# Attention scores as two 64-row products on their own halves of TensorE's rows, in place of one 128-row product with block-diagonal keys

## The chip, the cores and the metric

One NeuronCore of a Trainium2 chip runs the whole program in one launch. The metric is the time of one execution on the device in microseconds (us). The kernel before takes 1839.62 us, the median of 3 runs (1839.45 to 1840.44).

## The reference

Attention over 8 batches of 8 heads with keys and values averaged over groups of 8 positions, then two channel-mixing layers of width 512 to 2048 to 512. Only the attention scores are touched by the change.

```python
# B, H, S, D = 8, 8, 576, 64; pool = 8; Sp = 72
k_p = k.reshape(B, H, Sp, pool, D).mean(axis=3)
v_p = v.reshape(B, H, Sp, pool, D).mean(axis=3)
scores = scale * np.matmul(q, k_p.transpose(0, 1, 3, 2))     # per head: [576, 64] x [64, 72]
scores = scores - np.max(scores, axis=-1, keepdims=True)
attn = np.exp(scores)
attn = attn / (np.sum(attn, axis=-1, keepdims=True) + 1e-09)
x = np.matmul(attn, v_p)                                     # then heads side by side: [8, 576, 512]
h = x.transpose(0, 2, 1) @ U @ V
u = x + h.transpose(0, 2, 1)
x = u + np.maximum(u @ w_ch1, 0.0) @ w_ch2                   # first layer
...
out = x + np.maximum(norm(x) @ w_ch1, 0.0) @ w_ch2           # second layer
```

## The kernel before

The program has two parts. Phase A (`phase_a`) runs the attention of all 8 batches and, one batch behind it, half of the first layer's mixing (`a_l1`, L1015, and `a_l2`, L1047, 24 and 24 groups of main matmuls at L1027 and L1060, 288 columns each). Then three passes over 9 groups of 512 tokens run the rest of the mixing (matmuls at L1257 and L1345).

Attention goes by pairs of heads, 4 pairs per batch, 32 in all. The two heads of a pair lie one above the other: rows 0 to 63 of a tile are the 64 dimensions of the first head, rows 64 to 127 those of the second. For each pair `att_load` (L696) brings q, k and v; `att_prep` (L710) sums the keys over 8 positions into `kp` [128, 72], on VectorE (L718) or in three steps on GpSimd (L721, L722), and copies each head's half of `kp` into its own block of `kbd` [128, 2, 72], whose other blocks are zeros since the start (L494). The two copies run on ScalarE or VectorE. `att_s` (L759) then makes the scores of 128 queries with both heads in one product: 128 queries of both heads are the stationary operand (a weight load of 128 columns), `kbd` with its 144 columns streams past, and 128 x 144 scores land in PSUM (L767). Five such products make a pair, three in a first bank of the ring `py` and two in a second.

`att_m` (L775) takes the maxima (L789), scales them (L797), runs ten exponentials on ScalarE (L803) and divides by the sums. `att_t` (L820) turns the result back with TensorE transposes (L378): two blocks of four with 128 rows, and one of two with 64 rows, from rows 64 to 127, for the last 64 queries. `att_av` (L854) multiplies with the values (L871, or L889 and L890 from the third batch on). `att_xt` (L902) and `att_g` (L920) transpose the heads' outputs and multiply them with U (L927 and L928), in five steps of which the last has 64 rows only.

No order is written out by hand across engines. Every operation is recorded with the engines that can run it and its cost there, and `schedule` (L151) plays these through and hands out engine and place by due time; the program is emitted in that order and each engine then runs its own list in that order. For TensorE the due time is a running sum of planned costs. The scores' planned cost is one line:

```python
            {PE: 4 * 2 * SP / 2.4},
```

The ring `py` has 4 PSUM banks, and scores, transposes, the products with V, U and the rest of the attention share them. The rings `kbd`, `kp` and `q` have two tiles each.

Of the kernel before, what the change touches and what calls it, by code (L numbers as in the profile page):

```python
# [14 lines left out]
ALU = mybir.AluOpType  # L15
AX = mybir.AxisListType
# [7 lines left out]
SP = S // POOL  # L24
# [12 lines left out]
QT = [0, 128, 256, 384, 448]  # L37
# [54 lines left out]
PE, ACT, DVE, GP, SY = "pe", "act", "dve", "pool", "sync"  # L92
# [253 lines left out]
def c_dve(n):  # L346
    return 68 + 1.042 * n


def c_fast(n):  # L350
    return 68 + 0.521 * n


def c_act(n, ps=False):
    return (51 if ps else 93) + 0.8333 * n


def c_pool(n):
    return 147 + 2.11 * n
# [21 lines left out]
def copy(nc, e, dst, src):  # L381
    if e is nc.scalar:
        e.copy(dst, src)  # L383
    else:
        e.tensor_copy(dst, src)  # L385


class Kern:
    def __init__(self, nc, tc, aps):
        self.nc, self.tc = nc, tc  # L390
        (self.qT, self.kT, self.v, self.U, self.V, self.wA, self.g, self.wC, self.out) = aps
        self.w_raw = [self.wA, self.wC]
        self.o = Order(nc, tc)
        att = Pool("att")
        stg = Pool("stg")
        slots = Pool("slots", side="right")
        w = Pool("wres", side="right")
        b1 = Pool("b1", after=[att])
        b2 = Pool("b2", side="right", after=[w])
        ps = Pool("ps", space=PSUM)  # L400
        self.pools = [stg, att, slots, w, ps, b1, b2]
        R = self.R = {}

        def ring(pool, name, shape, dt=F32, n=1, fifo=True):
            R[name] = Ring(pool, shape, dt, n, name, fifo)

        ring(stg, "wraw", [128, 512], I64)
        ring(stg, "wx", [128, 512])
        ring(stg, "wt", [128, 512])
        ring(att, "araw", [128, 512], I64)  # L410
        ring(att, "ax", [128, 512])
        ring(att, "at", [128, 512])
        ring(att, "kbd", [128, 2, SP], n=2)
        ring(att, "q", [128, S], n=2)
        ring(att, "k", [128, S])
        ring(att, "v", [SP, 2, POOL * D])
        ring(att, "kp", [128, SP], n=2)
        ring(att, "vs", [SP, 4, D], F32R, 3)
        ring(att, "vz", [SP, 3 * D], n=2)
        ring(att, "ef", [SP, 2, S])  # L420
        ring(att, "sc", [128, 5, 2 * SP], n=2)
        ring(att, "mx", [128, 10], n=2)
        ring(att, "sm", [128, 10], n=2)
        ring(att, "eh", [SP, 2, S], F32R)
        ring(att, "el", [SP, 2, S], F32R)
        ring(att, "avt", [128, SH], n=2)
        ring(att, "xT", [128, S], n=5)
        ring(att, "xh", [128, DM], F32R, 2)
        ring(att, "xl", [128, DM], F32R, 2)
        ring(att, "gr", [128, DM], F32R)  # L430
        ring(att, "gs", [128, DM], F32R)
        ring(att, "ust", [128, 5, 128], F32R)
        ring(att, "vstk", [128, S], F32R)
        ring(slots, "op", [128, SLOT], F32R, 16)
        ring(slots, "hid", [128, SLOT], F32R, 8)
        for f in range(NA):
            for a in "hl":
                ring(w, f"w{a}{f}", [128, 1024], F32R)
        ring(w, "ys", [128, SH], n=2)
        for j in range(NSL):  # L440
            pool = b1 if j < NSL - 1 else b2
            for a in "hl":
                ring(pool, f"w1{a}{j}", [128, 7, 256], F32R)
                ring(pool, f"w2{a}{j}", [128, 2, 512], F32R)
        ring(b1, "xraw", [128, NCC, TG])
        ring(b1, "t3", [128, 2, TH])
        ring(b1, "t2", [128, 2, TH])
        ring(b2, "s12", [128, TG], n=2)
        ring(b2, "s5", [128, TH], n=2)
        ring(b2, "res", [128, NCC, TG], n=2)  # L450
        ring(b2, "yt", [128, NCC, TG])
        for a in ("lnh", "lnl"):
            ring(b2, a, [128, TH], F32R)
        for a in ("lns", "lnq", "lnm", "lnv", "lnd"):
            ring(b2, a, [128, TH])
        ring(ps, "pa", [128, 512], n=2)
        ring(ps, "pbc", [128, 512], n=2, fifo=False)
        ring(ps, "py", [128, 512], n=4)
# [31 lines left out]
                self.w_d[layer, f] = dp.tile([128, 1024], F32, tag=f"w_d{layer}_{f}", name=f"w_d{layer}_{f}")  # L490

    def setup2(self):
        for t in self.R["kbd"].tiles:
            self.nc.gpsimd.memset(t, 0.0)  # L494
        for t in self.R["vz"].tiles:
            self.nc.gpsimd.memset(t[:, D : 2 * D], 0.0)

# [212 lines left out]
    def att_prep(self, P):  # L710
        nc, o = self.nc, self.o
        q, k, v = self.raw[P]
        kp, kbd = self.buf("kp"), self.buf("kbd")
        kv = lambda: k.t.rearrange("p (n s) -> p n s", s=POOL)

        def pool(e):
            if e is nc.vector:
                e.tensor_reduce(kp.t, kv(), axis=AX.X, op=ALU.add)  # L718
                return
            for n in (4, 2):  # L720
                e.tensor_add(kv()[:, :, :n], kv()[:, :, :n], kv()[:, :, n : 2 * n])  # L721
            e.tensor_add(kp.t, kv()[:, :, 0], kv()[:, :, 1])  # L722

        o.op({DVE: c_dve(S), GP: c_pool(4 * SP) + c_pool(2 * SP) + c_pool(SP)}, pool, w=[k, kp])
        for h in range(2):
            r = slice(64 * h, 64 * h + 64)
            o.op(
                {ACT: c_act(SP), DVE: c_fast(SP)},
                lambda e, r=r, h=h: copy(nc, e, kbd.t[r, h], kp.t[r]),
                r=[kp],  # L730
                w=[(kbd, h)],
            )
        self.qk[P] = (q, kbd)

    def att_prep_v(self, P):
        o = self.o
# [20 lines left out]
        )  # L757

    def att_s(self, P, t):  # L759
        q, kbd = self.qk[P]  # L760
        if t in (0, 3):
            self.sps[P, t // 3] = self.buf("py")
        ps = self.sps[P, t // 3]
        i = t % 3 * 2 * SP
        self.o.op(
            {PE: 4 * 2 * SP / 2.4},
            lambda e: e.matmul(  # L767
                ps.t[:, i : i + 2 * SP], q.t[:, QT[t] : QT[t] + 128], kbd.t.rearrange("p h n -> p (h n)"),
                start=True, stop=True, skip_group_check=True,
            ),  # L770
            r=[q, kbd],
            w=[ps],
        )

    def att_m(self, P):  # L775
        nc, o = self.nc, self.o
        self.sc[P] = self.buf("sc")
        sb, mx, sm = self.sc[P], self.buf("mx"), self.buf("sm")
        sc = lambda: sb.t.rearrange("p t (h n) -> p (t h) n", h=2)
        bc = lambda t: t.rearrange("p (g o) -> p g o", o=1).to_broadcast([128, 10, SP])  # L780
        n = 10 * SP
        both = {GP: 1350, DVE: c_dve(n)}
        scale = 1.0 / (POOL * 8)
        for z, (g0, g1) in enumerate(((0, 6), (6, 10))):
            ps = self.sps[P, z]
            m = (g1 - g0) * SP
            o.op(
                {DVE: c_dve(m)},
                lambda e, ps=ps, g0=g0, g1=g1, m=m: e.tensor_reduce(  # L789
                    mx.t[:, g0:g1], ps.t[:, :m].rearrange("p (g n) -> p g n", n=SP), axis=AX.X, op=ALU.max  # L790
                ),
                r=[ps],
                w=[(mx, z)],
            )
            o.op(
                {DVE: 74, GP: 170},
                lambda e, g0=g0, g1=g1: e.tensor_scalar(mx.t[:, g0:g1], mx.t[:, g0:g1], -scale, None, op0=ALU.mult),  # L797
                w=[(mx, z)],
            )
            for g in range(g0, g1):  # L800
                o.op(
                    {ACT: 297},
                    lambda e, ps=ps, g=g, g0=g0: e.activation(  # L803
                        sc()[:, g],
                        ps.t[:, (g - g0) * SP : (g - g0 + 1) * SP],
                        AF.Exp,
                        bias=mx.t[:, g : g + 1],
                        scale=scale,
                        accum_out=sm.t[:, g : g + 1],
                    ),  # L810
                    r=[ps, (mx, z)],
                    w=[(sb, g), (sm, g)],
                )
        o.op(
            {DVE: 74}, lambda e: e.tensor_scalar(sm.t, sm.t, 1e-9, float(POOL), op0=ALU.add, op1=ALU.mult), w=[sm]
        )
        o.op({DVE: 131}, lambda e: e.reciprocal(sm.t, sm.t), w=[sm])
        o.op(both, lambda e: e.tensor_mul(sc(), sc(), bc(sm.t)), r=[sm], w=[sb])
# [788 lines left out]
```

## Time and profile before

| what | before |
|---|---|
| median of 3 runs | 1839.62 us (1839.45 to 1840.44) |
| profiled execution: its own time | 1839.23 us |
| profiled execution: span | 1837.4 us |
| TensorE matmul busy | 1769.2 us (96%), 11482 records |
| TensorE weight loads busy | 1619.5 us (88%) |
| VectorE busy | 1279.1 us (70%) |
| ScalarE busy | 723.4 us (39%) |
| GpSimd busy | 435.6 us (24%) |
| mean granted TensorE clock | 0.977 |
| the chain that ended last, by engine | PE 87%, DVE 9%, DMA 1%, ACT 1% |

PE is TensorE's matmul side and PEld its weight loads, DVE is VectorE, ACT ScalarE, POOL GpSimd. An f32 matmul instruction shows as two records on PE and two on PEld; one of another type as one. The end of a matmul record is modelled, and successive matmuls overlap in the records, so the length of a record (0.29 us for a score product) is not what it costs: that is read from how far the ends of successive records stand apart.

### The profile page before, as it was taken

How to read it: one execution, taken by the hardware profiler on the slowest of the kernel's cores; microseconds unless marked ns; L12 is line 12 of the kernel's file. 1: busy time of each engine (PE TensorE's matmuls, PEld its weight loads, DVE VectorE, ACT ScalarE, POOL GpSimd, SP SyncE). 2: the span in 40 equal slices, each digit the busy share in tenths (PEclk: the TensorE clock that was granted, in tenths of full speed). 3: DMA queues.
4: the chain of work that ended last, by engine and by line, in shares of the span. 5: the costliest groups of instructions: out<-in, count | busy, mean ns of one | idle time of the engine just before them, and what ended most of it. 6: DMA issues, size and time to landing. Idle time of an engine off the chain costs nothing.

```text
span 1837.4 us, 30175 instructions
## 1 busy us (share of the span) xinstructions
PE 1769.2 (96%) x11482; PEld 1619.5 (88%) x11482; DVE 1279.1 (70%) x2512; ACT 723.4 (39%) x2047; POOL 435.6 (24%) x446
## 2 busy tenths in 40 slices
PE   5689999999999999999999999999999999999999
PEld 4579999999999998888888888999999999999998
DVE  7987888888855577888888898776434754454443
ACT  4445655655644233333333453333332432222221
POOL 2242322323310122222222331111111321111110
PEclk7689999999999999999999999999999999999999
DMA  6434444444411352333333334434111433222211
GB/s 179 152 114 154 137 153 155 138 154 149 124 62 46 111 192 81 115 115 115 115 115 115 115 127 138 132 127 142 53 64 58 160 116 115 93 92 92 98 64 47
DMA packets 88642, 212.42 MB, mean 116 GB/s; under 512 B 9264, under 2 KB 17456, under 8 KB 82736
## 3 DMA queue, kind: packets, MB, share of 16 engines
q1 hardware_dynamic: 88352, 210.49, 34.8%
q8 instruction: 90, 1.47, 0.3%
q14 instruction: 56, 0.46, 0.1%
q10 hardware_dynamic: 144, 0.00, 0.0%
HBM read 141.25 MB, written 69.21 MB: 115 GB/s over the span
## 4 chain that ended last, share of the span: by engine, by line
PE 87%; DVE 9%; DMA 1%; ACT 1%; issue 1%; POOL 0%; SPq 0%; DVEq 0%; ACTq 0%; POOLq 0%
PE py L1345 30%; PE pa L1257 15%; PE pbc L1257 12%; PE pa L1027 11%; PE pbc L1060 10%; PE py L378 3%; PE py L767 2%; PE py L871 1%; DVE lnv L1468 1%; DVE res L1481 1%; DVE lnd L1466 1%; PE py L889 1%; PE py L890 1%; PE py L928 0%; DMA v<-v 0%
## 5 line engine op out<-in xcount | busy, mean ns | idle before, releaser
L1345 PE MATMUL py<-hid,w2h 128*128 128x512 f32 x1728 | 546.4, 398 | 0.0
L1257 PE MATMUL pa<-op,w1h 128*128 128x256 f32 x1728 | 328.5, 282 | 21.5 <-DVE pa L1321 19.8
L1257 PEld LDWEIGHTS pa<-op,w1h 128*128 128x128 f32 x1728 | 294.0, 189 | 59.4 <-DVE pa L1321 22.6
L1345 PE MATMUL py<-hid,w2l 128*128 128x512 f32 x864 | 337.9, 391 | 0.0
L1345 PEld LDWEIGHTS py<-hid,w2h 128*128 128x128 f32 x1728 | 278.7, 191 | 13.4
L1257 PE MATMUL pbc<-op,w1h 128*128 128x256 f32 x1296 | 247.2, 283 | 1.3 <-ACT s L383 0.6
L1257 PEld LDWEIGHTS pbc<-op,w1h 128*128 128x128 f32 x1296 | 221.9, 190 | 28.5 <-DVE lnv L1465 0.8
L1257 PE MATMUL pa<-op,w1l 128*128 128x256 f32 x864 | 244.2, 283 | 0.0
L1027 PE MATMUL pa<-hid,wh 128*128 128x288 f32 x1024 | 220.1, 307 | 8.9 <-DVE op L1039 8.8
L1060 PE MATMUL pbc<-op,wh 128*128 128x288 f32 x1024 | 215.8, 303 | 0.0
L1315 DVE TENSOR_TENSOR pbc<-s,pbc 128x512 f32<-128x512 f32 x108 | 74.8, 692 | 183.2 <-PE pbc L1257 183.1
L1345 PEld LDWEIGHTS py<-hid,w2l 128*128 128x128 f32 x864 | 163.4, 189 | 36.6
L1257 PE MATMUL pbc<-op,w1l 128*128 128x256 f32 x648 | 183.7, 283 | 0.0
L1027 PEld LDWEIGHTS pa<-hid,wh 128*128 128x128 f32 x1024 | 167.1, 192 | 12.3 <-DVE op L1039 8.7
L1279 ACT ACTIVATE hid<-pbc 128x512 fp32r<-128x512 f32 x108 | 64.7, 599 | 266.4 <-DVE pbc L1315 265.6
L1060 PEld LDWEIGHTS pbc<-op,wh 128*128 128x128 f32 x1024 | 163.7, 188 | 4.4 <-issue 2.8
L1257 PEld LDWEIGHTS pa<-op,w1l 128*128 128x128 f32 x864 | 163.4, 189 | 0.0
L1027 PE MATMUL pa<-hid,wl 128*128 128x288 f32 x512 | 153.3, 299 | 0.4 <-POOL wl L508 0.4
L1060 PE MATMUL pbc<-op,wl 128*128 128x288 f32 x512 | 150.9, 295 | 0.0
L383 ACT COPY s<-pa 128x256 f32<-128x256 f32 x200 | 74.3, 372 | 146.3 <-PE pa L1257 144.1
L508 POOL TENSOR_TENSOR op<-t,op 128x512 fp32r<-128x512 f32 x26 | 35.2, 1356 | 393.0 <-DVE op L385 312.5
L1279 ACT ACTIVATE hid<-pa 128x512 fp32r<-128x512 f32 x108 | 64.5, 597 | 156.3 <-PE pa L1257 149.4
(189 smaller groups left out, 3135.3 us busy)
## 6 DMA issues: line engine op xcount, KB each, us to landing
xraw<-n_d SPq DMA_DIRECT2D x18, 1024.0 KB, 4.8
wraw<-wC SPq DMA_DIRECT2D x32, 512.0 KB, 4.1
wraw<-wA SPq DMA_DIRECT2D x24, 512.0 KB, 4.3
w_d<-wx SPq DMA_DIRECT2D x48, 256.0 KB, 4.0
wraw<-w_d SPq DMA_DIRECT2D x48, 256.0 KB, 3.7
k<-kT SPq DMA_DIRECT2D x32, 288.0 KB, 3.7
q<-qT SPq DMA_DIRECT2D x32, 288.0 KB, 3.2
v<-v SPq DMA_DIRECT2D x32, 288.0 KB
```

The lines of the kernel that those rows point to most:

```text
L378: e.matmul(out, src, ident, start=first, stop=True, is_transpose=True, skip_group_check=True)
L383: e.copy(dst, src)
L508: lambda e: e.tensor_sub(lo(), src(), hi().bitcast(F32)),
L767: lambda e: e.matmul(ps.t[:, i : i + 2 * SP], q.t[:, QT[t] : QT[t] + 128], kbd.t.rearrange("p h n -> p (h n)"), start=True, stop=True, ski ...
L871: lambda e: e.matmul(ps.t[:, :SH], vs.t[:, w], ef.t[:, h, c], start=(h == 0), stop=(h == 1)),
L889: e.matmul(ps.t[:, :SH], w, eh.t[:, h, c], start=True, stop=False)
L1027: e.matmul(ps.t[:, :SH], w.t[:, c], u, start=(i == 0), stop=(i == 3 * NCC - 1))
L1060: e.matmul(ps.t[:, :SH], w.t[:, c], x, start=(f == 0 and j == 0), stop=(f == NA - 1 and j == 2))
L1257: e.matmul(bank.t[:, sl], w.t[:, self.WCOL[k], c], u.t[:, t], start=(first and i == 0), stop=(last and i == 5), skip_group_check=True,)
L1279: lambda e: e.activation(h.t[:, :TG], bank.t, AF.Relu),
L1315: o.op({DVE: c_dve(TG)}, lambda e: e.tensor_add(c.t, s.t, c.t), r=[s], w=[c])
L1345: e.matmul(y.t, w.t[:, i, c], x.t[:, :TG], start=(first and q == 0), stop=(last and q == 2))
```

## The change

The zero blocks and the copies into them go. `att_s` issues two products for each 128 queries, one per head. Each has the head's 64 rows of q as its stationary operand (still 128 columns) and the head's 64 rows of `kp` as the streaming one (72 columns), the second head's on rows 64 to 127 of TensorE. The two heads write into two different banks, both taken from the ring at the pair's first product, so that a bank holds the five blocks of one head and not three or two blocks of both heads. `att_m` reads them so: each bank's maxima go to every second column of `mx`. The planned cost of a score product becomes 3 * 72 / 2.4 = 90 ns, two of them 180 ns, where one of 240 ns stood.

```diff
-        ring(att, "kbd", [128, 2, SP], n=2)
...
     def setup2(self):
-        for t in self.R["kbd"].tiles:
-            self.nc.gpsimd.memset(t, 0.0)
...
-        kp, kbd = self.buf("kp"), self.buf("kbd")
+        kp = self.buf("kp")
...
-        for h in range(2):
-            r = slice(64 * h, 64 * h + 64)
-            o.op(
-                {ACT: c_act(SP), DVE: c_fast(SP)},
-                lambda e, r=r, h=h: copy(nc, e, kbd.t[r, h], kp.t[r]),
-                r=[kp],
-                w=[(kbd, h)],
-            )
-        self.qk[P] = (q, kbd)
+        self.qk[P] = (q, kp)
...
     def att_s(self, P, t):
-        q, kbd = self.qk[P]
-        if t in (0, 3):
-            self.sps[P, t // 3] = self.buf("py")
-        ps = self.sps[P, t // 3]
-        i = t % 3 * 2 * SP
-        self.o.op(
-            {PE: 4 * 2 * SP / 2.4},
-            lambda e: e.matmul(
-                ps.t[:, i : i + 2 * SP], q.t[:, QT[t] : QT[t] + 128], kbd.t.rearrange("p h n -> p (h n)"),
-                start=True, stop=True, skip_group_check=True,
-            ),
-            r=[q, kbd],
-            w=[ps],
-        )
+
+        q, kp = self.qk[P]
+        if t == 0:
+            self.sps[P] = self.buf("py"), self.buf("py")
+        for h, ps in enumerate(self.sps[P]):
+            r = slice(64 * h, 64 * h + 64)
+            self.o.op(
+                {PE: 3 * SP / 2.4},
+                lambda e, r=r, ps=ps: e.matmul(
+                    ps.t[:, t * SP : t * SP + SP], q.t[r, QT[t] : QT[t] + 128], kp.t[r],
+                    start=True, stop=True, skip_group_check=True,
+                ),
+                r=[q, kp],
+                w=[ps],
+            )
...
-        for z, (g0, g1) in enumerate(((0, 6), (6, 10))):
-            ps = self.sps[P, z]
-            m = (g1 - g0) * SP
+        for z in range(2):
+            ps = self.sps[P][z]
+            m = 5 * SP
...
-                    mx.t[:, g0:g1], ps.t[:, :m].rearrange("p (g n) -> p g n", n=SP), axis=AX.X, op=ALU.max
+                    mx.t[:, z:10:2], ps.t[:, : 5 * SP].rearrange("p (g n) -> p g n", n=SP), axis=AX.X, op=ALU.max
...
-            for g in range(g0, g1):
+            for g in range(z, 10, 2):
...
-                        ps.t[:, (g - g0) * SP : (g - g0 + 1) * SP],
+                        ps.t[:, g // 2 * SP : (g // 2 + 1) * SP],
```

Lines of the changed program from `att_s` on stand ten lower: the scores are L757, the main matmuls L1017 and L1050. On TensorE 160 score instructions become 320. The three places that follow show how they stand among the others; `hid` is a batch's input to the mixing, `wh` and `wl` its weights, `sc` the exponentials of a pair, `pa` and `pbc` the mixing's banks.

TensorE, a pair in the third batch, its last two score products and what stands around them, before:

```order
L767 MATMUL py_235<-kbd_144,q_146 128x144
L1060 MATMUL pbc_234<-op_197,wh_222 128x288 x2
L1060 MATMUL pbc_234<-op_197,wl_223 128x288
L1060 MATMUL pbc_234<-op_198,wh_224 128x288 x2
L1060 MATMUL pbc_234<-op_198,wl_225 128x288
L378 MATMUL py_237<-ident,sc_157 72x128 x4
L767 MATMUL py_235<-kbd_144,q_146 128x144
L1060 MATMUL pbc_233<-op_191,wh_210 128x288 x2
```

The same place in the changed program:

```order
L757 MATMUL py_233<-kp_148,q_144 128x72
L757 MATMUL py_234<-kp_148,q_144 128x72
L1050 MATMUL pbc_232<-op_195,wh_220 128x288 x2
L1050 MATMUL pbc_232<-op_195,wl_221 128x288
L1050 MATMUL pbc_232<-op_196,wh_222 128x288 x2
L1050 MATMUL pbc_232<-op_196,wl_223 128x288
L378 MATMUL py_235<-ident,sc_155 72x128 x4
L757 MATMUL py_233<-kp_148,q_144 128x72
L757 MATMUL py_234<-kp_148,q_144 128x72
L1050 MATMUL pbc_231<-op_189,wh_208 128x288 x2
```

One score product between 128-row work has become two 64-row ones that stand together, one per head.

TensorE, a later pair in the changed program, where the second head's products do not stand beside the first's:

```order
L757 MATMUL py_233<-kp_148,q_144 128x72
L378 MATMUL py_234<-ident,sc_155 72x128 x4
L757 MATMUL py_233<-kp_148,q_144 128x72 x2
L1017 MATMUL pa_230<-hid_201,wh_210 128x288
L1017 MATMUL pa_230<-hid_202,wh_210 128x288
L1017 MATMUL pa_230<-hid_201,wl_211 128x288
```

Here four transposes of 128 rows have moved in between the products of one head.

VectorE, the first rows of the program, before:

```order
L718 TENSOR_REDUCE kp_149<-k_147 128x72
L385 COPY kbd_143<-kp_149 64x72 x2
L747 TENSOR_TENSOR v_148<-v_148 72x2x256
L789 TENSOR_REDUCE mx_159<-py_235 128x6
L797 TENSOR_SCALAR mx_159<-mx_159 128x6
L789 TENSOR_REDUCE mx_159<-py_236 128x4
L797 TENSOR_SCALAR mx_159<-mx_159 128x4
```

and in the changed program:

```order
L715 TENSOR_REDUCE kp_147<-k_145 128x72
L736 TENSOR_TENSOR v_146<-v_146 72x2x256
L736 TENSOR_TENSOR v_146<-v_146 72x2x128
L779 TENSOR_REDUCE mx_157<-py_233 128x5
L779 TENSOR_REDUCE mx_157<-py_234 128x5
L787 TENSOR_SCALAR mx_157<-mx_157 128x5
L542 TENSOR_SCALAR at_142<-araw_140 128x512
```

The copies into `kbd` are gone from VectorE here, and one of the two scalings of the maxima has moved to GpSimd. Over the program 25 such copies leave VectorE and 39 leave ScalarE, and of the 32 sums of keys 20 now stand on GpSimd, 12 on VectorE (10 and 22 before).

## Rows read from the trace of the kernel before

**Rows 1.** Engines by stretch: us, busy (instructions) PE, PEld, DVE, ACT, POOL, clock, DMA, GB/s

```profile
0.00:140.00 140.00, 99.72 (x484) 83.44 (x485) 121.28 (x288) 64.46 (x262) 43.12 (x53) 0.77 0.49 147
140.00:600.00 460.00, 458.56 (x3406) 441.73 (x3405) 361.89 (x808) 252.60 (x912) 119.79 (x150) 1.00 0.41 128
600.00:1150.00 550.00, 527.22 (x3327) 478.61 (x3326) 442.89 (x807) 209.06 (x466) 152.57 (x147) 0.98 0.36 121
```

**Rows 2.** Waits of PE, 140 to 600 us (all): total us, times, longest us

```profile
PE py L928 <- DVE xl L508: 1.3, 3, 0.5
```

**Rows 3.** Waits of PE, 0 to 140 us, the three longest

```profile
PE py L378 <- DVE sc L818: 13.1, 3, 9.9
PE pa L1027 <- DVE op L1039: 8.8, 3, 5.9
PE py L767 <- DVE kbd L385: 5.0, 1, 5.0
```

**Rows 4.** Score products, 140 to 575 us: records, ns min/median/max, first and last start

```profile
L767 PEld LDWEIGHTS py<-kbd,q x232: 187/189/193, 141.0 to 559.5; 128*128 128x128 f32 x116
L767 PE MATMUL py<-kbd,q x232: 283/286/288, 141.1 to 559.6; 128*128 128x144 f32 x116
```

**Rows 5.** Timeline of PE around one score product: start us, us, what

```profile
202.53 0.29 PE L890 MATMUL py<-el,vs 72*128 72x288 f32 x1
202.66 0.41 PE L767 MATMUL py<-kbd,q 128*128 128x144 f32 x2
202.81 0.52 PE L1027 MATMUL pa<-hid,wh 128*128 128x288 f32 x2
203.17 0.29 PE L1027 MATMUL pa<-hid,wl 128*128 128x288 f32 x1
```

**Rows 6.** Timeline of PE, products with U on 128 rows

```profile
218.10 0.29 PE L1060 MATMUL pbc<-op,wl 128*128 128x288 f32 x1
218.23 0.40 PE L927 MATMUL py<-xh,ust 128*128 128x512 f32 x1
218.47 0.39 PE L928 MATMUL py<-xl,ust 128*128 128x512 f32 x1
218.69 0.60 PE L378 MATMUL py<-ident,xT 128*128 128x128 f32 x4
```

**Rows 7.** Timeline of PE, the same products on 64 rows

```profile
224.50 0.29 PE L1060 MATMUL pbc<-op,wl 128*128 128x288 f32 x1
224.72 0.50 PE L927 MATMUL py<-xh,ust 64*128 64x512 f32 x1
225.05 0.39 PE L928 MATMUL py<-xl,ust 64*128 64x512 f32 x1
225.38 0.53 PE L1060 MATMUL pbc<-op,wh 128*128 128x288 f32 x2
225.74 0.29 PE L1060 MATMUL pbc<-op,wl 128*128 128x288 f32 x1
```

**Rows 8.** Timeline of PE, transposes from rows 64 to 127

```profile
207.20 0.41 PE L767 MATMUL py<-kbd,q 128*128 128x144 f32 x2
207.54 0.30 PE L378 MATMUL py<-ident,sc 64*72 64x64 f32 x2
207.78 0.53 PE L1027 MATMUL pa<-hid,wh 128*128 128x288 f32 x2
208.14 0.29 PE L1027 MATMUL pa<-hid,wl 128*128 128x288 f32 x1
```

**Rows 9.** Copies into kbd, 0 to 140 us

```profile
L383 ACT COPY kbd<-kp x14: 247/249/254, 11.5 to 124.3; 64x72 f32<-64x72 f32 x14
L385 DVE COPY kbd<-kp x6: 181/192/196, 4.5 to 26.4; 64x72 f32<-64x72 f32 x6
```

**Rows 10.** Engines by stretch, as rows 1; and the longest wait of PE from 600 to 1150 us

```profile
750.00:800.00 50.00, 47.45 (x284) 42.59 (x285) 41.86 (x74) 18.29 (x42) 14.61 (x16) 0.95 0.38 127
...
PE pa L1257 <- DVE pa L1321: 19.8, 10, 2.4
```

More of the change, by code (lines that the diff above doesn't have):

```diff
@@ L783, in att_m @@
         scale = 1.0 / (POOL * 8)
-        for z, (g0, g1) in enumerate(((0, 6), (6, 10))):
-            ps = self.sps[P, z]
-            m = (g1 - g0) * SP
+        for z in range(2):
+            ps = self.sps[P][z]
+            m = 5 * SP
             o.op(
                 {DVE: c_dve(m)},
-                lambda e, ps=ps, g0=g0, g1=g1, m=m: e.tensor_reduce(
-                    mx.t[:, g0:g1], ps.t[:, :m].rearrange("p (g n) -> p g n", n=SP), axis=AX.X, op=ALU.max
+                lambda e, ps=ps, z=z: e.tensor_reduce(
+                    mx.t[:, z:10:2], ps.t[:, : 5 * SP].rearrange("p (g n) -> p g n", n=SP), axis=AX.X, op=ALU.max
                 ),
@@ L796, in att_m @@
                 {DVE: 74, GP: 170},
-                lambda e, g0=g0, g1=g1: e.tensor_scalar(mx.t[:, g0:g1], mx.t[:, g0:g1], -scale, None, op0=ALU.mult),
+                lambda e, z=z: e.tensor_scalar(mx.t[:, z:10:2], mx.t[:, z:10:2], -scale, None, op0=ALU.mult),
                 w=[(mx, z)],
             )
-            for g in range(g0, g1):
+            for g in range(z, 10, 2):
                 o.op(
                     {ACT: 297},
-                    lambda e, ps=ps, g=g, g0=g0: e.activation(
+                    lambda e, ps=ps, g=g: e.activation(
                         sc()[:, g],
-                        ps.t[:, (g - g0) * SP : (g - g0 + 1) * SP],
+                        ps.t[:, g // 2 * SP : (g // 2 + 1) * SP],
                         AF.Exp,
```

## The prediction

> **What bounds the kernel now.** I read the engines by stretch first [rows 1]. From 140 to 600 us TensorE is busy 458.56 of 460 us at a clock of 1.00; the same stretch shows VectorE at 362 and GpSimd at 120 us. Busy matmul records overlap, so the list of TensorE's waits must confirm it: in these 460 us it names one group of 1.3 us in all [rows 2]. So in this stretch whatever a score product costs TensorE more or less comes out at the end, one for one. Before 140 us it is otherwise: TensorE is busy 100 us at a clock of 0.77, VectorE 121, and TensorE waits mostly for VectorE [rows 3]. From 600 to 1150 us TensorE idles 23 of 550 us [rows 1].
>
> Next, what a score product costs. Records are 0.286 us long [rows 4], but their ends stand closer. From the end of L890 (202.53 + 0.29 = 202.82) to the end of the last main product (203.17 + 0.29 = 203.46) lie 0.64 us [rows 5]; three main products take 0.13 each (203.33 to 203.46 is one), which leaves 0.25 for the score instruction, 0.125 for each of its two records.
>
> Last, what 64 rows cost among 128-row work, which this kernel already has in two places. The two products with U take 0.47 us on 128 rows (ends 218.39 to 218.86) [rows 6]. On 64 rows the span from the end of the product before them (224.79) to the end of the third main product behind (226.03) is 1.24 us [rows 7]; take off 0.47 and 3 x 0.13 and 0.38 us are left over. The records show where: L927 ends 0.43 after its forerunner and not 0.24, and the main products behind stand 0.2 late. The two 64-row transposes show the same: from 207.61 to 208.43 are 0.82 us [rows 8]; less 0.39, and less 0.11 for two transposes of 64 columns (one of 128 columns takes 0.11: four end 0.43 after L928 [rows 6]), 0.32 us are left. Their weight load has 72 columns, that of L927 128, as the new score products have. So entering and leaving 64-row work costs TensorE 0.32 to 0.38 us each time, however much stands between.
>
> By the Trainium skill, page TensorEngine Tiling (Array Packing), Key Properties, changing the tiling mode drains TensorE, while another tile of the same mode does not. The 0.38 us agree with the first half; no run here yet shows the second.
>
> **The change part by part.** *Switches.* In the changed order I count runs of neighbouring 64-row products from the 193rd main product on, which is where the records of rows 4 begin. Before there are 33 (25 begin with transposes, 8 with a product with U or its correction): 25 x 0.32 + 8 x 0.38 = 11.0 us. After there are 122, of which 96 begin with a score, 18 with transposes, 8 with the others: 104 x 0.38 + 18 x 0.32 = 45.3 us. That is **+34.2 us**, all of it on TensorE's solid stretch. Score products that stand together share one switch, which is why it is 122 and not 230.
>
> *The products themselves.* In this stretch 117 score instructions become 230, each two records: 234 x 0.125 = 29.3 us become 460 records. If streaming sets their pace, 72 columns take half of 144, 0.0625 us: 28.8 us in all, -0.5. If the weight load sets it, the nearest row is the transposes with loads of 128 columns, 0.11 us apart [rows 6]; that row's streaming alone could set 0.11, so it is an upper bound. The first load of each of the 96 runs lies inside the switch, so 96 x 0.0625 + 364 x 0.11 = 46.0 us, +16.7. If the second record of one head runs beside the first of the other (they own different rows and banks), a pair of instructions takes three places of four: 21.6 us, -7.7. I take 0.085 us, half way between streaming and load, since neither row decides: 6.0 + 30.9 = 36.9, **+7.6 us**.
>
> By the Trainium skill, page TensorE: Matmul & The Clock Gate, section LDWEIGHTS, a weight load's time goes by its columns, whatever its rows, at 1/1.2 ns each: an estimate of 107 ns here, which makes the sum of the loads much like the bound just named; rows 6 do not contradict it.
>
> *Before 140 us* 17 runs stand where 8 stood: 9 x 0.38 is 3.4 us at the full clock and 6.8 at the half. TensorE is only part of what bounds this stretch, so perhaps half of that counts. Against it, 6 copies of 0.19 us leave VectorE and 14 of 0.25 leave ScalarE [rows 9], and the first scores start two copies, 0.4 us, earlier. Some sums of keys move from VectorE to GpSimd, which is busy 43 of 140 us. I take **+1 us**, between -5 and +7; the upper end includes a longer share at the half clock.
>
> *Copies after 140 us, the zero fills, the maxima:* nothing. VectorE has 98 and ScalarE 207 us free in the stretch, and TensorE waits for neither [rows 1, 2]. The cover would have to go before these count. Two maxima of 360 columns replace 432 and 288, the same total.
>
> *Banks.* A pair now holds two of the four `py` banks from its first product on; before, the second was taken at the fourth product. Waits on a free bank are fixed by the order and can appear in TensorE's list, which has next to none now [rows 2]. Bounds: nothing, or 0.3 us for each of the 23 pairs in the stretch, 7 us. I take nothing and keep 7 for the range. *The passes:* of the 7200 matmuls from the first L1257 on, all but 12 keep their place. Nothing, give or take 3 us for VectorE's work in another order.
>
> Sum: 34.2 + 7.6 + 1 = 42.8 us on the profiled execution's 1839.23 (0.4 us under the median of 1839.62, and 1.8 over its span): **1882 us**.
>
> **The rivals.** *Overlap.* The heads' products run side by side, with the switches as priced: 34.2 - 7.7 + 1 = 27.5, **1867 us**. For it: different rows and different banks. Against: the loads still have 128 columns each. By the Trainium skill, TensorE: Matmul & The Clock Gate, Part 3, matmuls on different row groups run at the same time; no row here has two such neighbours.
>
> *Each change of head drains too.* The changed order has 87 places in the stretch where a 64-row product follows one on the other half. If each costs half a switch, 0.19 us, that is 16.5 more: **1899 us**. For it: entering on rows 64 and on rows 0 both cost the same in rows 7 and 8. Against: neither row shows a change between halves.
>
> *The clock falls.* From 750 to 800 us the granted clock is 0.95, that is, part of the time at 1.2 GHz in place of 2.4, where TensorE has single waits up to 2.4 us [rows 10]. If 500 us of phase A ran so, 0.05 x 500 = 25 us more: **1907 us**. Against: the new gaps are 0.2 us each, and from 140 to 600 us, with the 33 switches there, it is 1.00 [rows 1].
>
> *Faster.* What rows 7 and 8 show is not the 64 rows but something of those two places (a wait, a transpose next to a product), and score runs cost no switch; with overlap -7.7 and -1 from the start are left: **1830 us**. It decides where a switch costs under 0.1 us (8.7 us over 89 more runs). Against: two different kinds of product, in every instance, with no wait listed. That the heads sit on their own halves but run one after the other is no case of its own; it is the dearer end of the forecast.
>
> **How the numbers follow.** My forecast, 1882 us, has 0.60; its own range is 1869 to 1897 by the cost of a record and of the banks. Overlap 0.14, draining between heads 0.12, the clock 0.05, faster 0.05, and 0.04 for what I do not see, half of it within the measurement. The range 1862 to 1905 takes in the forecast, overlap and draining between heads, with the early bound on either side, and leaves the rest out. A measurement of this kernel can tell about 0.2% (3.7 us) from no change; faster 0.05, same 0.02, slower 0.93.
>
> **What would show it.** Right: between two main products a pair of score products takes some 0.65 to 0.8 us where one took 0.25, the first main product behind ends 0.2 late, and phase A's last main products come about 42 us later while the passes keep their length. The waits of TensorE from 140 to 640 us stay at a few us. The pace of neighbouring score records tells 0.0625 from 0.11, and the ends at a change of head show or refute a drain there. It would be wrong if score runs stood among main products without a gap, if the waits for `py` banks came to more than 10 us, or if the clock of the stretch were under 0.98.

## The result and the profile after

The changed kernel takes 1866.2 us (median of 4 runs, 1863.46 to 1868.13); the kernel before, run beside it, 1839.53. The ratio is 1.0148 (95% interval 1.0126 to 1.0171): slower by 1.5%, some 27 us. That lies inside the range of 1862 to 1905, but well under the forecast of 1882 and under the forecast's own 1869 to 1897, and almost on the 1867 that stood for the heads running side by side. The profiled execution took 1868.13 us, its span is 1866.3 us where 1837.4 stood.

The profile after, engines by stretch (columns as in [rows 1]):

```profile
0.00:140.00 140.00, 106.57 (x590) 86.73 (x590) 120.14 (x283) 63.29 (x260) 39.39 (x53) 0.94 0.49 148
140.00:600.00 460.00, 460.00 (x3394) 425.31 (x3393) 332.39 (x748) 236.41 (x854) 126.68 (x161) 1.00 0.39 122
600.00:1150.00 550.00, 529.09 (x3375) 482.57 (x3374) 435.43 (x797) 213.14 (x479) 148.33 (x145) 0.98 0.35 117
```

Against [rows 1]: from 140 to 600 us TensorE's records now cover all of the 460 us, but its weight loads fell from 441.73 to 425.31 although there are more score products; VectorE does 332 us of work where it did 362. The list of TensorE's waits from 140 to 640 us is empty, so no other engine holds it up there. The clock is 1.00 in this stretch as before. The 0.94 of the first row is no gain over the 0.77 before; the part on the first 140 us below says why.

Where the time went, by the place of the main matmuls on TensorE (their starts in the two profiles):

| stretch | before | after | difference |
|---|---|---|---|
| start to the 193rd main matmul of phase A | 135.35 us | 133.7 us | -1.7 us |
| from there to its last main matmul | 517.0 us | 549.6 us | +32.6 us |
| from there to the end (the passes) | 1185.1 us | 1183.1 us | -2.0 us |

The middle stretch can be taken apart by the ends of successive matmul records, as the prediction does at single places: for each record, how far its end stands behind the end of the one before it. What exceeds the product's own pace at the first 64-row product of a run and at the first 128-row product behind it is the switch.

| from the 193rd to the last main matmul | before | after | difference |
|---|---|---|---|
| runs of 64-row products | 33 | 122 | +89 |
| switches, in and out | 11.3 us | 45.4 us | +34.1 us |
| the score products' own pace | 28.7 us (234 records) | 30.5 us (460) | +1.8 us |
| all the rest | 477.0 us | 473.7 us | -3.3 us |

So the loss is in the switches, 45.4 / 122 = 0.37 us each, in and out together. The line between switch and pace is a convention, the prediction's own: of the first score record of a run 0.06 us count as pace and the rest as switch; with 0.11 us some 5 us would move from the switches to the products. One switch, with two products in it, in the timeline of TensorE after (start us, us, what):

```profile
242.96 0.30 PE L1050 MATMUL pbc<-op,wl 128*128 128x288 f32 x1
243.19 0.45 PE L757 MATMUL py<-kp,q 64*128 64x72 f32 x4
243.56 0.54 PE L1050 MATMUL pbc<-op,wh 128*128 128x288 f32 x2
243.94 0.29 PE L1050 MATMUL pbc<-op,wl 128*128 128x288 f32 x1
```

From the end of the first row (243.26) to the end of the last (244.23) are 0.97 us; three main products at 0.13 take 0.39, so the scores of 128 queries take 0.58 us where one 128-row instruction took 0.25 [rows 5]. The four records themselves are done 0.38 us after the product before them, of which some 0.2 is entering; the main products behind come 0.2 late, as in [rows 7].

And this one, where only one head's product stands between 128-row work:

```profile
238.91 1.17 PE L757 MATMUL py<-kp,q 64*128 64x72 f32 x14
240.01 0.63 PE L378 MATMUL py<-ident,sc 128*72 128x128 f32 x4
240.57 0.44 PE L757 MATMUL py<-kp,q 64*128 64x72 f32 x2
240.94 0.53 PE L1050 MATMUL pbc<-op,wh 128*128 128x288 f32 x2
```

Two records end 0.37 us after the transposes before them (240.64 to 241.01); four records of both heads above took 0.38. The second head comes almost free: that is the overlap. The first row is another run of scores; it ends at 240.08, the four transposes behind it at 240.64. Of these 0.56 us they take 0.11 each themselves, so leaving cost 0.12 us here and not 0.2.

### The profile page after: what moved, and what is told of

The parts are those of the page before. It is cut to its first block, busy times and chain, and to the rows that moved or that the text cites. A ratio compares the mean times of both kernels' runs of the same rounds, so it can differ in the third digit from the quotient of the medians.

```text
span 1866.3 us, 30831 instructions
## 1 busy us (share of the span) xinstructions
PE 1808.3 (97%) x11802; PEld 1636.7 (88%) x11802; DVE 1263.5 (68%) x2483; ACT 719.4 (39%) x2018; POOL 438.6 (24%) x458
## 4 chain that ended last, share of the span: by engine, by line
PE 88%; DVE 9%; DMA 1%; ACT 1%; issue 1%; POOL 0%; SPq 0%; DVEq 0%; ACTq 0%; POOLq 0%
PE py L1335 30%; PE pa L1247 15%; PE pbc L1247 12%; PE pbc L1050 11%; PE pa L1017 11%; PE py L757 3%; PE py L378 3%; DVE res L1471 1%; DVE lnv L1458 1%; PE py L879 1%; DVE lnd L1456 1%; PE py L880 1%; DMA v<-v 1%; PE py L917 1%; PE py L918 0%
## 5 line engine op out<-in xcount | busy, mean ns | idle before, releaser
L1017 PE MATMUL pa<-hid,wh 128*128 128x288 f32 x1024 | 217.6, 305 | 1.9 <-DVE op L1029 1.9
L1050 PE MATMUL pbc<-op,wh 128*128 128x288 f32 x1024 | 216.1, 303 | 0.0
L1017 PEld LDWEIGHTS pa<-hid,wh 128*128 128x128 f32 x1024 | 164.8, 191 | 7.0 <-DVE op L1029 2.8
L1050 PEld LDWEIGHTS pbc<-op,wh 128*128 128x128 f32 x1024 | 163.6, 189 | 7.4 <-issue 2.8
L1017 PE MATMUL pa<-hid,wl 128*128 128x288 f32 x512 | 151.7, 296 | 0.0
L1050 PE MATMUL pbc<-op,wl 128*128 128x288 f32 x512 | 151.1, 295 | 0.0
```

Source lines behind the costliest of these rows:

```text
L1017: e.matmul(ps.t[:, :SH], w.t[:, c], u, start=(i == 0), stop=(i == 3 * NCC - 1))
L1050: e.matmul(ps.t[:, :SH], w.t[:, c], x, start=(f == 0 and j == 0), stop=(f == NA - 1 and j == 2))
```

## The experiments

All were run beside the kernel before. Where a difference is given it is against the median of those runs: 1834.84 us for two products on 128 rows, ten together, the heads apart and the transposes on 128 rows, 1835.75 for those run beside the second run of the change. The last one, the kernel before again, is a single run.

**The change again.**

> The change itself, beside the others on one chip: 27 us over the kernel before (24 to 30) by every theory.

1864.48 us against 1835.75, ratio 1.0162 (1.0147 to 1.0177), 28.7 us over. Its profile repeats the table above: 45.4 us of switches in 122 runs, 30.5 us for the products, 549.6 us for the stretch.

**Two products, but on 128 rows.** The edit brings back `kbd`, its zero fill and its copies, and changes the product:

```diff
-                lambda e, r=r, ps=ps: e.matmul(
-                    ps.t[:, t * SP : t * SP + SP], q.t[r, QT[t] : QT[t] + 128], kp.t[r],
+                lambda e, h=h, ps=ps: e.matmul(
+                    ps.t[:, t * SP : t * SP + SP], q.t[:, QT[t] : QT[t] + 128], kp.t[:, h],
```

where `kp` now names the `kbd` tile that `att_prep` hands over.

> The changed kernel with its two products per 128 queries and its two banks, but on all 128 rows again: the zero-filled keys and the copies into them are back, and each product streams one head's 72 columns of them. Theory one (every run of 64-row products costs TensorE some 0.37 us at its ends, and the two heads run side by side): from the 193rd main product on the runs of 64-row products fall from 122 to 33, so 34 us of gaps go, but 460 score records without any overlap stand 0.11 us apart, 51 us in place of 30.5: about 1855 us (1848 to 1862), and no gap at either end of a score product. Theory two (what costs is the doubled number of products, the banks and the order, not the rows): as the change, 1866 us (1862 to 1870), with gaps around the products.

1863.43 us, ratio 1.0156 (1.0141 to 1.0171), 28.6 us over. By its total this looks like theory two and no different from the change, and it lies outside theory one's 1848 to 1862. The timeline says otherwise (line 768 is the score, line 1028 a main product):

```profile
205.55 0.29 PE L1028 MATMUL pa<-hid,wl 128*128 128x288 f32 x1
205.68 0.56 PE L768 MATMUL py<-kbd,q 128*128 128x72 f32 x4
206.04 0.51 PE L1028 MATMUL pa<-hid,wh 128*128 128x288 f32 x2
...
220.73 0.30 PE L1061 MATMUL pbc<-op,wl 128*128 128x288 f32 x1
220.87 0.34 PE L768 MATMUL py<-kbd,q 128*128 128x72 f32 x2
```

The first score record follows the product before it at once (205.68 is 0.13 behind 205.55; in the change it was 0.23). Four records end 0.40 us after that product (205.84 to 206.24), two records 0.18 (221.03 to 221.21): on the same rows each further record costs 0.11 us, whichever head it belongs to, where on different halves the second head's two cost 0.01 together. Over the middle stretch the switches are back at 11.7 us, the products' own pace is 47.1 us where the change has 30.5, and the stretch takes 538.8 us, 21.8 over the kernel before, 10.7 under the change. Theory one's two terms come out (34 us of switches less, 33.7 measured; 51 us of products, 47.1 measured); some 6 us of other gaps that it did not have came back. What its total missed lies ahead of the stretch: the first main product of phase A starts at 97.8 us, where it was 77.5 before and 78.7 in the change, and the 193rd at 143.4, where it was 135.35 and 133.7. The cause there (the copies are back, and the order is another) was not separated. So theory two falls by the missing gaps, and a total alone would have misled.

**Ten products together.** All ten products of a pair become one operation:

```diff
+        if t:
+            return
...
-        for h, ps in enumerate(self.sps[P]):
-            r = slice(64 * h, 64 * h + 64)
-            self.o.op(
...
+        def mm(e, bs=self.sps[P]):
+            for i, h in [(i, h) for i in range(5) for h in range(2)]:
+                r = slice(64 * h, 64 * h + 64)
+                e.matmul(
+                    bs[h].t[:, i * SP : i * SP + SP], q.t[r, QT[i] : QT[i] + 128], kp.t[r],
+                    start=True, stop=True, skip_group_check=True,
+                )
+
+        self.o.op({PE: 10 * 3 * SP / 2.4 + 390}, mm, r=[q, kp], w=list(self.sps[P]))
```

> The changed kernel with all ten score products of a pair recorded as one operation, heads taking turns, so that they stand together; the scheduler may hand two banks to one operation. Products, rows, banks and copies are those of the change. Runs of 64-row products from the 193rd main product on fall from 122 to 56. Theory one: 66 runs x 0.37 = 24.6 us go, and a pair's ten products take 1.08 us (0.061 and then 9 steps that come to 0.224 per product of both heads), 24.8 us in the stretch in place of 30.5: about 1836 us (1831 to 1842). Theory two: products and banks are as before, so 1866 us (1861 to 1871).

1842.89 us, ratio 1.0043 (1.0028 to 1.0058), 8.0 us over the kernel before, so some 20 us of the 28 are gone with the same products on the same rows. In the middle stretch the switches fall from 45.4 to 20.5 us (56 runs, 0.37 each again), and the products' pace from 30.5 to 24.7 us, under the 28.7 of the kernel before; both are as expected. The total lies just above the expected 1831 to 1842, because small gaps grew: switches and products together gave 30.7 us, but the stretch takes 526.4 us, only 23.2 less than in the change, so some 7.5 us were given back between other products. Of these 3.1 us are three listed waits of a main product for VectorE (L1032), where the change has none. One run of ten (line 761 is the score):

```profile
233.17 0.29 PE L1053 MATMUL pbc<-op,wl 128*128 128x288 f32 x1
233.39 1.34 PE L761 MATMUL py<-kp,q 64*128 64x72 f32 x20
234.66 0.54 PE L1053 MATMUL pbc<-op,wh 128*128 128x288 f32 x2
```

Twenty records end 1.27 us after the product before them (233.46 to 234.73). The change has runs of five products of one head, ten records:

```profile
268.19 0.29 PE L880 MATMUL py<-el,vs 72*128 72x288 f32 x1
268.41 1.33 PE L757 MATMUL py<-kp,q 64*128 64x72 f32 x10
269.67 0.53 PE L1050 MATMUL pbc<-op,wh 128*128 128x288 f32 x2
```

They end after 1.26 us (268.48 to 269.74). Twenty of two heads take what ten of one take.

**The heads apart.** The same, with one line in another order:

```diff
-            for i, h in [(i, h) for i in range(5) for h in range(2)]:
+            for i, h in [(i, h) for h in range(2) for i in range(5)]:
```

> As the run with ten together, but the five products of the first head stand before the five of the second. Runs stay at 56. If neighbouring products of the two heads run side by side, this loses it: 20 records 0.112 us apart are 2.19 us for a pair in place of 1.08, 25.5 us more over the 23 pairs of the solid stretch: about 1862 us (1857 to 1870). If heads don't overlap and the short steps in the records are only how ends are modelled: the same as with ten together, within 4 us.

1859.47 us, ratio 1.013 (1.0108 to 1.0152), inside the expected range: 16.6 us over ten together, by an edit of the order of the ten alone. A run now looks so:

```profile
239.90 0.29 PE L1053 MATMUL pbc<-op,wl 128*128 128x288 f32 x1
240.13 2.06 PE L761 MATMUL py<-kp,q 64*128 64x72 f32 x20
242.12 0.54 PE L1053 MATMUL pbc<-op,wh 128*128 128x288 f32 x2
```

Twenty records end after 2.00 us (240.19 to 242.19) in place of 1.27. Expected were 2.39 with entering; the ends of single records show why it is less: around the change of head about eight of them still stand 0.05 to 0.06 apart, so the second head's first products run beside the first head's last. The products' pace in the stretch is 41.3 us, 16.6 more than with heads in turn. That this equals the difference of the medians is chance: the stretch as a whole takes 538.8 us, 12.4 more, since other gaps shrank, and the 193rd main product comes 6.2 us later. So heads overlap only where they stand close.

**The transposes on 128 rows.** In the kernel before, with the scores left alone:

```diff
-                    e4 = sc.t[64:, 4, h * SP : h * SP + SP]
-                    turn(e, ps.t[:SP, h * 64 : h * 64 + 64], e4, self.ident[64:, 64:], h == 0)
+                    turn(e, ps.t[:SP, h * 128 : h * 128 + 128], sc.t[:, 4, h * SP : h * SP + SP], self.ident, h == 0)
...
-            src = lambda t: t[:SP, :128].rearrange("p (h n) -> p h n", h=2)
+            src = lambda t: t[:SP, :256].rearrange("p (h n) -> p h n", h=2)[:, :, 64:]
```

> The kernel before with one edit: the two 64-row transposes of each pair turn all 128 rows of the last block, and only the last 64 columns are copied out. Score products are untouched. Theory one: 25 of the 33 runs of 64-row products in the solid stretch go, 25 x 0.32 = 8.0 us, and 50 transposes cost 0.11 in place of 0.055 us, 2.7 us: 5.3 us less, about 1834 us (1831 to 1837). If the gaps belong to that place and not to the 64 rows: 2.7 us more, 1842 us (1840 to 1845).

1830.16 us, ratio 0.9972 (0.9961 to 0.9983): 4.7 us less, near the 5.3. But the profile does not put the gain where it was expected. The switches did fall from 11.3 to 3.1 us, the transposes cost 2.7 more, and yet the middle stretch takes 516.1 us, only 0.8 less: gaps between products, the scores' among them, took back 4.7 us. The 193rd main product comes at 128.6 us in place of 135.35; that is where most of the gain lies, and the cause of it (fewer switches, or the other order that the scheduler made) was not separated.

**No 64 rows at all.** In addition, in `att_g`:

```diff
-            e.matmul(pg.t, self.ust.t[:n, i], xh.t[:n], start=(i == 0), stop=False)
-            e.matmul(pg.t, self.ust.t[:n, i], xl.t[:n], start=False, stop=(i == 4))
+            e.matmul(pg.t, self.ust.t[:, i], xh.t, start=(i == 0), stop=False)
+            e.matmul(pg.t, self.ust.t[:, i], xl.t, start=False, stop=(i == 4))
```

> The kernel before with no 64-row product left in the solid stretch but one: the transposes of the last block turn 128 rows, as in the run before, and the fifth product with U runs on 128 rows too (the rows of U behind its end are zeros, the other operand holds older finite values there). Runs of 64-row products fall from 33 to 1. Theory one: to the 4.7 us that the transposes alone gave come 7 switches of 0.39, 2.7 us: 7.4 us less than the kernel before (5.5 to 9). If switches were not what counts: as with the transposes alone, 4.7 less.

1830.09 us, ratio 0.997 (0.996 to 0.998), 5.7 us less than the kernel before, at the low end of theory one's 5.5 to 9: the fastest version found, by a little. Its middle stretch takes 513.7 us, 2.4 under the run with the transposes alone, as 7 switches should give (2.7). In the total the two can't be told apart, nor does the total decide between theory one and the 4.7 of the other; the stretch does.

**Ten together, and no other 64 rows.** Both edits on the run with ten together.

> Ten score products together, heads taking turns, and no other 64-row product: runs fall from 56 to 24 in the solid stretch. Theory one: 32 x 0.37 = 11.8 us less than with ten together alone, 2.7 us more for the longer transposes: 9.1 us less, that is 1 us under the kernel before (4 under to 3 over). Theory two (products and banks cost, not switches): as with ten together, 8 us over the kernel before.

1831.48 us, ratio 0.9978 (0.9968 to 0.9988), 4.3 us less than the kernel before and so 12.3 better than ten together; expected were 9.1. It is just past theory one's 4 us under the kernel before. The runs fall from 56 to 24, the switches from 20.5 to 9.5 us, and the stretch from 526.4 to 515.3 us, where theory two expected no change. So 64-row scores with heads in turn are no loss once a pair needs one switch, but they are no gain either over 128 rows without any switch (1830.09 us, and 513.7 in the stretch).

**The copies kept.** The change, with the copies into `kbd` still made for nobody.

> The change, with the copies of each head's keys still made into a tile that nobody reads (the zero fill is left out). The prediction put the removed copies at nothing in the solid stretch: as the change, within 3 us. If they had paid for a part of the loss: more than 3 us over the change.

1868.51 us, ratio 1.0185 (1.0168 to 1.0202), a median 4.0 us over the change, but the two intervals overlap and the profiled executions stand the other way round (spans 1863.3 and 1864.5 us; one is the fastest of its four, the other the slowest). Inconclusive for the total. In the middle stretch the copies cost nothing (548.1 us against 549.6); they may cost some microseconds at the start, where the 193rd main product comes at 136.0 us, in the change's second profile at 132.7.

**The kernel before again.**

> The kernel before once more, for a second profile of it: the runs of it beside the experiments lie from 1833 to 1839.5 us, and the profile on which the prediction rests is one of 1839.2. If the spread comes from the first 140 us, where that profile has a clock of 0.77, then a profile some 4 us shorter passes its 193rd main product earlier by as much, with a higher clock before it, and takes the same 517 us from there to the last main product of phase A (516 to 518). If it comes from elsewhere, the 193rd main product comes at 135 us again.

1836.4 us, and the first of the two cases is refuted, the second holds. The 193rd main product comes at 135.35 us again, with a clock of 0.78 before 140 us; the middle stretch takes 516.4 us, and it is the passes that are shorter, 1182.9 us in place of 1185.1. So in these two profiles the start is the same, and 2 us more or less in the passes need no change to explain them.

## Why the prediction was right, and where it was off

The direction, the stretch and the price of the switches were right; the pace of the products was mis-sized, and the total fell in the range by way of the rival that stood beside the forecast.

- **The bound.** Right. TensorE sets the end in the middle stretch one for one: its +32.6 us in the middle stretch, less 1.7 before and 2.0 behind, are the 28.9 by which the spans differ.
- **Switches, +34.2 us.** Measured +34.1, in 122 runs as counted in the order. The price read from two places of the trace before, 0.32 to 0.38, held for a third kind of product: 0.37. The kernels with the same products in fewer runs show it as well (56 runs 20.5 us, 24 runs 9.5 us). An agreement to 0.1 us is closer than the split allows, since the convention for the first record alone moves 5 us.
- **The products themselves, +7.6 us.** This is the step that failed: "I take 0.085 us, half way between streaming and load, since neither row decides". There is no one pace. Records of one head stand 0.11 apart, the value called the upper bound, and their weight loads end as far apart; the run on 128 rows, with the same loads and 72 columns, has 0.11 too, where half the pace of the 144-column product would be 0.06. So the load sets it by these rows; no run changed the load's columns alone. Records of the other half run beside them and add 0.01. A pair of products that stand together takes 0.06 + 0.01 + 0.105 + 0.01 = 0.18 us behind the switch. With single heads and longer runs mixed in, the whole is 30.5 us, +1.8.
- **Before 140 us, +1 us.** Measured -1.7 to the 193rd main product. TensorE still waits mostly for VectorE:

```profile
PE py L378 <- DVE sc L808: 11.5, 3, 9.6
PE py L757 <- DVE kp L715: 5.1, 1, 5.1
PE py L757 <- DMA q<-qT: 4.8, 1, 4.8
```

  The first answers to the first of [rows 3] (13.1). The third is the wait before the first score product, 5.0 us in [rows 3]: without the two copies it starts 0.2 us earlier, in the change's second profile 0.4, which is what the prediction counted. The second is the wait for the keys of the second pair, 4.4 us before. The clock did not help: the change's profile has no record of the clock ahead of 66 us, that of the kernel before none ahead of 17 us, and such time counts as full clock in the rows. The products show otherwise, eight transposes on either side of 66 us in the change:

```profile
62.37 1.92 PE L378 MATMUL py<-ident,xT 128*128 128x128 f32 x8
67.20 1.03 PE L378 MATMUL py<-ident,xT 128*128 128x128 f32 x8
```

  In the change all transposes on 128 rows from 14.8 to 64 us end 0.21 us apart, as they do in the kernel before where its clock is recorded at half (1.2 GHz), and those behind 66 us 0.11. With the time ahead of the first record taken at half, the two means for 140 us are 0.70 and 0.71, an estimate from these rows, in place of 0.94 and 0.77. What made the 1.7 us was not separated.
- **Banks, nothing to 7 us; the passes, nothing.** The 0.3 us a pair behind the 7 was taken from no row. No wait appeared in the middle stretch; on the contrary 3.3 us of small gaps went. The passes' -2.0 is within what two profiles of the kernel before differ.
- **The rivals.** Overlap was the right one, at a chance of 0.14: its 27.5 us and the measured 26.7 are close, but it took three places of four for the products, 21.6 us; the products took 30.5, and the small gaps, the start and the passes gave back what it had not counted. That its total came so near is in part luck. By the Trainium skill, TensorE: Matmul & The Clock Gate, Part 3, matmuls on different row groups run at the same time. The runs agree: in turn, twenty records of two heads took the 1.27 us that ten of one head take. A drain at each change of head falls: the steps there are 0.01 us, and with ten together a pair changes heads nine times for one switch. By the Trainium skill, TensorEngine Tiling (Array Packing), Key Properties, changing the tiling mode drains TensorE, and changing only the tile does not. Both halves now agree, with 0.37 us for the first and 0.01 us for the second; what the 0.37 us consist of no run separated. The clock did not fall (1.00 from 140 to 600 us), and the case of no switch cost falls with the switches.
- **The signs.** A pair of score products took 0.58 us between main products, under the 0.65 to 0.8 that was called right; the main product behind ended 0.2 late, as called; phase A's last main product came 30.9 us later and not 42; the passes kept their length within 2.0 us.

In sum: the forecast was 42.8 us, the two profiles differ by 28.9. Of the 13.9 too much, 5.8 are the products' pace, 3.3 the small gaps, 2.7 the start, 2.0 the passes, and 0.1 the switches.

## What to carry to other kernels

Count how often TensorE goes from 128-row to 64-row work and back before halving a product: here each return trip cost 0.37 us, more than the 0.25 us of the product it was to shorten, and with 128 columns of weights a 64-row product of one head on its own was hardly cheaper than a whole one for both (0.22 us, two records 0.11 apart, against 0.25). Two halves come near to paying only when they stand close to each other in turn and many in a run. Even then they did not pay here: a pair's ten in one run took 1.27 us and 0.20 for leaving, where five whole products take 1.23. 64-row pieces that are not needed may be worth padding to 128 rows; here that gave 0.3%, though only part of it where the switches went. And read the stretch, not the total: two kernels here lost 28.6 and 28.7 us for different reasons.

## What the runs showed that was not expected

Weight loads of two row halves overlap as the products do: twenty loads of two heads in turn, each of 128 columns, took 1.19 us on PEld, ten of one head 1.19 too. The overlap reaches across some distance in the order: with five products of one head before five of the other, about eight records around the change still stood 0.05 to 0.06 us apart, and the run took 2.00 us in place of 1.27.

The number of products between does not matter to the price of a switch (leaving cost 0.20 us after two 64-row records and after twenty), but the first weight load behind it does. In the middle stretch of the kernels here, by medians, entering costs 0.20 us where the first 64-row product loads 128 columns (scores, products with U) and 0.12 where it loads 72 (transposes); leaving costs 0.20 us into products that load 128 columns and 0.12 into transposes, which load 72. So 0.37 us is an average over the changed kernel's switches, and the 0.38 and 0.32 us of [rows 7] and [rows 8] differ by this. It suggests that the price is in good part that one load, which isn't hidden behind other work at a switch; this was read from the ends of the records, and no run tested it.
